# A planned attention-and-MLP kernel: the plan charges VectorE and GpSimd for each other, costs as measured alone, a rank for every unit

## The chip, the cores and the metric

The kernel runs on one core of one Trainium2 chip. The metric is device time in microseconds of one execution; the kernel before was timed three times, with a median of 592.93 us (591.24 to 593.26). The engines are named as the profile names them: PE (TensorE), DVE (VectorE), ACT (ScalarE), POOL (GpSimd), SP (SyncE, which issues the DMAs). PEld is the loading of weights into PE.

## The reference

Attention over 4 batches, 8 heads, 768 positions and 64 channels, with a window of 96 keys and 8 global keys, and then a token-mixing and a channel-mixing MLP.

```python
scores = scale * np.matmul(q, k.transpose(0, 1, 3, 2))
bias = -slopes[:, None, None] * dist[None, :, :]
scores = np.where(keep, scores + bias[None], -1000000000.0)
a = np.exp(scores - np.max(scores, axis=-1, keepdims=True))
a = a / (np.sum(a, axis=-1, keepdims=True) + 1e-09)
x = np.matmul(a, v)            # then heads side by side: (4, 768, 512)
h = np.maximum(xt @ w_tok1, 0.0) @ w_tok2      # xt: x with positions last
u = x + h.transpose(0, 2, 1)
out = u + np.maximum(u @ w_ch1, 0.0) @ w_ch2
```

## The kernel before, in words

All work is cut into units, each for one engine, and a planner writes the order of the units on every engine before the program is built. The program then runs that order: on each engine an instruction follows the one ahead of it in the list (`InOrder`), whatever the others do. The planner (`Plan.record`) goes through time event by event; when an engine is free it gives it, of the units whose predecessors are done and whose buffers and PSUM banks are free, the one with the lowest rank. Each unit carries a cost in microseconds per engine that may do it; where a unit may go to two or three engines, the first that is free takes it. So costs and ranks set two things: the order on each engine, and which engine does a unit that several may do.

The units, with the names of the plan, which the text uses:

- **Attention**, `pair(v)`, v = 0 to 47, 12 for each batch: two heads and 256 positions. `load` (DMA into a ring of four buffers, `e` in the trace), `q` (scaling of the queries), `S` (scores on PE, `sp`), `max` (DVE), `exp` (ACT), `sum` and `inv`, `norm` (POOL, some on DVE), then for v below 20 `T` (transposes on PE, `tp`) and `back` (copy out of PSUM, ACT or DVE), above that `split` (DVE), `turn` (a transposing DMA) and `join`; `V` (values on PE, `op`) and `put` (ACT or DVE). From v = 16 on the load of unit v waits for V of unit v-4, whose buffer it takes.
- **Weights**, `weights(n)`, n = 0 to 29, 64-bit numbers that are turned into a high and a low float: `w` (DMA), `bits` and `down` (ACT), `shift` and `sign` (DVE, rows `t<-w,t`), `high` (ACT), `low` (DVE or POOL, rows `wc<-t,wc`). Only three pieces can be between `bits` and `low` at a time, for they share three buffers (`t`). `w0` to `w5` are for the token MLP, the rest for the channel MLP.
- **Token MLP** of batch b, `tokens(b)`: `N` (transposes, `xtp`), `nh`, `nl`, `J` (`pj`), `jh` (ACT), `jl` (DVE), `U` 0 to 7 (`pu`), `ua` (DVE), `uh` (ACT), `ul` (DVE or POOL). U of batch 0 needs `jl`, and `low3` to `low5`.
- **Channel MLP**, `channel(q)` in chunks of 512 positions with twelve steps each: `F` k (12 matmuls, `hp`), `fh` (ACT, `hh`), `fl` (DVE, `hl`), `g` k in two halves of 6 matmuls (`acc`). This is the dense work, in three matmuls for each product of split floats; the last two chunks are done together in `last()` with fewer products (`P`, `G`, `H`).

Dense work of one batch is laid between the attention units of the next. PSUM has eight banks of 512 floats: `g` holds four, `F` one until `fl` is done, `S`, `T` and `V` two each.

The lines that set the order: the call in `record` that adds a unit's cost (line 212 of the profile's numbering), the `add` calls with their costs in `weights`, `pair`, `tokens` and `channel`, and `rank` with its tables at the end. Before, a rank is a straight line for each kind, as in

```python
    if kind == "pair":
        v = at[0]
        b, i = divmod(v, PER)
        if b == 0:
            return 10.0 * v
        return PAIRS[b - 1][0] + PAIRS[b - 1][1] * i
```

All compute instructions of the trace bear line 235 (`InOrder.__getattr__`), so the rows are told apart by tile names.

Of the kernel before, what the change touches and what calls it, by code (L numbers as in the profile page):

```python
# [22 lines left out]
B, H, S, D = 4, 8, 768, 64  # L23
# [17 lines left out]
FIRST = 3  # L41
PER = H // 2 * NU
# [82 lines left out]
class Plan:  # L125
# [118 lines left out]
class Fast:  # L244
# [68 lines left out]
    def weights(self, n):  # L313
# [5 lines left out]
        add, dve, act = self.plan.add, self.dve, self.act  # L319
# [39 lines left out]
        add(f"w{n}", "sp", 1.85, load, [f"w{n - 1}"] if n else [], rank("load weights", n), ["w", "raw"])  # L359
        add(f"bits{n}", "act", 0.7, bits, [f"w{n}"], r, ["t"])  # L360
        add(f"down{n}", "act", 0.64, down, [f"bits{n}"], r)
        add(f"shift{n}", "dve", 0.73, shift, [f"down{n}"], r)
        add(f"sign{n}", "dve", 0.76, sign, [f"shift{n}"], r, (), ["w", "raw"])
# [38 lines left out]
    def pair(self, v):  # L402
# [130 lines left out]
            if v == FIRST - 1:  # L533
                add("branch", "sp", 0.1, lambda: None, [f"load{v}"], -100)
        if v:
            add(f"q{v}", dict(dve=0.3, act=0.4, pool=0.56) if b == 0 else dict(pool=0.56), 0, lambda e: self.scale(v, e),
                [f"load{v}"], r - PRI['q'])
        wp = ["w"] if wide else ["p", "p"]

# [6 lines left out]
        add(f"sum{v}", *(("pool", 0.37) if FIRST <= v < PER else ("dve", 0.2)), sums, [f"exp{v}0", f"exp{v}1"], r - PRI["sum"])  # L546
        add(f"inv{v}", "dve", 0.16, inverses, [f"sum{v}"], r - PRI["sum"])
        for e in range(2):
            add(f"norm{v}{e}", dict(dve=0.6, pool=1.04) if v < FIRST or PER - 3 <= v < PER else dict(pool=1.4 if b == 1 else 1.04),
                0, lambda en, e=e: norm(e, en), [f"inv{v}"], r - PRI["norm"])  # L550
        if not far:
            add(f"T{v}", "pe", 0.75, transposes, [f"norm{v}0", f"norm{v}1"], r - PRI["T"],
# [4 lines left out]
            late, give = "back", wp + (["w"] if FIRST <= v < PER else [])  # L557
        else:
            for e in range(2):
                add(f"split{v}{e}", "dve", 0.67, lambda e=e: split(e), [f"norm{v}{e}"] + ([f"split{v}0"] if e else []), r - PRI["split"],  # L560
                    [] if e else ["mix", "mix"])
                add(f"turn{v}{e}", "sp", 1.3, lambda e=e: turned(e), [f"split{v}{e}"], -1000)
                add(f"join{v}{e}", dict(act=1.06, dve=0.69), 0, lambda en, e=e: join(e, en), [f"turn{v}{e}"], r - PRI["join"], (), ["p"])
            late, give = "join", ["mix", "mix"]
        add(f"V{v}", "pe", 0.7, values, [f"{late}{v}0", f"{late}{v}1"], r - PRI["V"],
            [("op", v, 0), ("op", v, 1)] + (["w"] if v < H // 2 else ["x"] if b and j == 0 else []), give, "quarters")
        for i in range(2):
            add(f"put{v}{i}", dict(act=0.24, dve=0.25), 0, lambda en, i=i: put(i, en), [f"V{v}"], r - PRI["put"], (), [("op", v, i)])


    def tokens(self, b):
# [83 lines left out]
        for i in range(4 * len(segs)):  # L655
# [10 lines left out]
            add(f"ul{b}{i}", dict(dve=0.12 + w / 900) if b == B - 1 else dict(pool=0.1 + w / 410, dve=0.12 + w / 900), 0, lambda en, i=i: low_u(i, en), [f"uh{b}{i}"],  # L666
                k - PRI['mix'], (), ([] if b == B - 1 else ["x"] if b else ["w"]) if end else [])


    def channel(self, q):  # L670
# [328 lines left out]

def rank(kind, *at):

    if kind == "weights":
        return WEIGHTS[0] + WEIGHTS[1] * at[0] if at[0] < 6 else WEIGHTS[2] + WEIGHTS[3] * at[0]
    if kind == "load weights":
        n = at[0]
        return LOADS[0] + LOADS[1] * n if n < 8 else LOADS[2] + LOADS[3] * n
    if kind == "load":
        return 2.5 * at[0]  # L1010
    if kind == "pair":
        v = at[0]
        b, i = divmod(v, PER)
        if b == 0:
            return 10.0 * v
        return PAIRS[b - 1][0] + PAIRS[b - 1][1] * i
    if kind == "mix":
        b, k = at
        if b == 0:
            return -20.0 + k  # L1020
        return MIXES[b - 1] + 2.5 * k
# [5 lines left out]
LOADS = [10.58, 4.16, 407.44, 1.08]
CHANNEL = [176.2, 6.52]
PAIRS = [(119.72, 6.24), (217.78, 12.78), (353.61, 5.31)]
PRI = {'q': -16.6, 'max': 27.3, 'exp': -7.0, 'sum': 90.7, 'norm': -19.4, 'T': -22.4, 'back': 52.4, 'split': -95.1, 'join': 5.2, 'V': 13.2, 'put': 25.2, 'F': 7.0, 'mix': -9.7, 'hid': 49.7, 'high': 21.0}  # L1030
# [253 lines left out]
```

## Time and profile before

| | before |
|---|---|
| median of 3 runs | 592.93 us |
| the profiled execution | 593.89 us |
| its span, first to last instruction | 592.0 us |
| PE busy | 567.0 us (96%) |
| DVE, ACT, POOL busy | 356.9, 276.2, 234.4 us |
| mean granted TensorE clock | 0.994 |
| moved by DMA | 62.47 MB |

The profile is one execution; the time around its span (593.89 less 592.0) is 1.89 us. A unit's time is found in the trace by its tile name and its place in the order. In a row of the timeline the second number is the time from the start of the first to the end of the last merged instruction; in brackets stands how long the engine had been idle and who released it.

### The profile page before, as it was taken

To read this page: it belongs to the slowest core of one execution; us is meant where nothing else is said; L and a number is where in the kernel's file an instruction comes from. 1 tells how busy PE (TensorE), PEld (TensorE's weight loads), DVE (VectorE), ACT (ScalarE), POOL (GpSimd) and SP (SyncE) were. 2 spreads that over 40 slices of the span, in tenths; PEclk is the share of its full clock that TensorE was granted. 3 is DMA by queue.
4 is the path that set the end of the run, shared out by engine and by line. 5 is a ranking of instruction groups with operands and counts; after the bars stand their busy time and mean duration, and the time that the engine had idled before them with its cause. 6 is when DMAs were issued, how large, how long until landed. Compare 5 with 4: busy or idle time off the path is not lost. (4 is left out here: it accounts for less than half of the span.)

```text
span 592.0 us, 11933 instructions
## 1 busy us (share of the span) xinstructions
PE 567.0 (96%) x4420; PEld 460.4 (78%) x4420; DVE 356.9 (60%) x952; ACT 276.2 (47%) x743; POOL 234.4 (40%) x377
## 2 busy tenths in 40 slices
PE   4989989998999999999999999999999999999995
PEld 2877868777888778788888877787887888888884
DVE  5999998989345664365422487567459755554400
ACT  5999978878433545132322255656244222222000
POOL 3888777656404532060300365344532144410000
PEclk9999999998999999999999999999999999999998
DMA  7990656782301674335420029675100100000201
GB/s 262 372 396 13 224 192 184 260 248 66 92 0 73 115 185 119 45 111 162 69 79 0 1 53 228 158 178 80 29 2 1 71 1 0 1 1 2 77 33 40
DMA packets 62435, 62.47 MB, mean 106 GB/s; under 512 B 46880, under 2 KB 50336, under 8 KB 62368
## 3 DMA queue, kind: packets, MB, share of 16 engines
q1 hardware_dynamic: 62224, 61.62, 36.3%
q8 instruction: 37, 0.61, 0.4%
q14 instruction: 30, 0.25, 0.1%
q10 hardware_dynamic: 144, 0.00, 0.0%
HBM read 44.30 MB, written 6.29 MB: 85 GB/s over the span
## 5 line engine op out<-in xcount | busy, mean ns | idle before, releaser
L235 PE MATMUL acc<-hh,wc 128*128 128x512 f32 x480 | 152.1, 398 | 0.0
L235 PE MATMUL hp<-uh,wc 128*128 128x512 f32 x432 | 144.8, 394 | 0.0
L235 PEld LDWEIGHTS acc<-hh,wc 128*128 128x128 f32 x480 | 88.2, 189 | 21.2 <-issue 2.8
L235 PEld LDWEIGHTS hp<-uh,wc 128*128 128x128 f32 x432 | 81.1, 188 | 18.4 <-ACT x L235 0.6
L235 PE MATMUL acc<-hl,wc 128*128 128x512 f32 x240 | 94.3, 393 | 0.2 <-DVE hl L235 0.2
L235 POOL TENSOR_SCALAR p<-p,st 128x192 f32<-128x192 f32 (+1 forms) x132 | 73.5, 572 | 38.9 <-DVE st L235 19.4
L235 PE MATMUL hp<-ul,wc 128*128 128x512 f32 x216 | 84.3, 390 | 0.0
L235 DVE COPY r<-p 128x768 uint16<-128x768 uint16 x84 | 56.3, 676 | 44.9 <-DMA p<-r 23.0
L235 ACT ACTIVATE hh<-hp 128x512 fp32r<-128x512 f32 x54 | 32.1, 594 | 83.8 <-PE hp L235 82.0
L235 DVE SCALAR_TENSOR_TENSOR hl<-hp,hh 128x512 fp32r<-128x512 f32 x54 | 36.9, 683 | 52.2 <-ACT hh L235 52.0
L235 POOL TENSOR_SCALAR e<-e,sc 128x256 f32<-128x256 f32 x37 | 21.4, 580 | 104.4 <-DMA e<-pk 95.9
L235 ACT ACTIVATE p<-p,st 128x192 f32<-128x192 f32 (+1 forms) x132 | 57.4, 439 | 11.1 <-DVE st L235 11.1
L235 PEld LDWEIGHTS acc<-hl,wc 128*128 128x128 f32 x240 | 45.2, 188 | 10.5 <-DVE hl L235 0.9
L235 DVE SCALAR_TENSOR_TENSOR t<-w,t 128x512 int32<-128x512 int32 x60 | 50.9, 857 | 2.6 <-POOL wc L235 1.3
L235 ACT COPY r<-p 128x768 uint16<-128x768 uint16 x28 | 29.8, 1066 | 37.2 <-DMA p<-r 31.9
L235 PEld LDWEIGHTS hp<-ul,wc 128*128 128x128 f32 x216 | 40.6, 188 | 7.9
L235 PE MATMUL sp<-e 64*64 64x192 f32 (+1 forms) x624 | 33.9, 337 | 12.4 <-ACT e L235 6.1
L235 DVE CUSTOM_DVE_ANT_0 p<-sp,bias 128x192 f32<-128x192 f32 (+1 forms) x132 | 37.3, 342 | 5.3 <-PE sp L235 5.0
L235 PEld LDWEIGHTS sp<-e 64*64 64x64 f32 x624 | 22.6, 141 | 18.8 <-ACT e L235 6.7
L235 PE MATMUL acc<-hid,wc 128*128 128x512 f32 x144 | 33.0, 389 | 0.0
L235 POOL TENSOR_TENSOR o<-uh,ul 128x512 f32<-128x512 f32 x16 | 22.6, 1429 | 25.3 <-DMA out<-o 17.1
L235 POOL TENSOR_TENSOR ul<-x,uh 128x512 fp32r<-128x512 f32 (+1 forms) x14 | 16.2, 1165 | 40.1 <-ACT uh L235 37.5
(145 smaller groups left out, 977.6 us busy)
## 6 DMA issues: line engine op xcount, KB each, us to landing
e<-pk SPq DMA_DIRECT2D x24, 592.0 KB, 4.3
w<-wc SPq DMA_DIRECT2D x24, 512.0 KB, 5.7
e<-pk SPq DMA_DIRECT2D x14, 560.0 KB, 5.0
unit<-pk SPq DMA_DIRECT2D x9, 384.0 KB, 6.2
w<-w SPq DMA_DIRECT2D x6, 512.0 KB, 7.0
out<-o SPq DMA_DIRECT2D x12, 256.0 KB, 2.1
keys<-pk SPq DMA_DIRECT2D x8, 208.0 KB, 5.7
out<-o SPq DMA_DIRECT2D x8, 128.0 KB, 1.8
```

The source lines that it names most:

```text
L235: ins = getattr(self.engine, name)(*args, **kw)
```

## The change

Four things in the planner, and none in what the units do. (1) A unit that starts on DVE while POOL runs one, or the other way round, is charged an extra time (`extra`), if both are in a list of units that share a way to SBUF. (2) The costs of some forty units are replaced: DVE `shift` 0.73 to 0.71, `sign` 0.76 to 0.71, `split` 0.67 to 0.58, POOL `low` 1.45 to 1.33, `norm` 1.04 or 1.4 to 0.88 or 0.98, `base` 1.42 to 1.32, and so on. (3) `rank` takes a number for each unit from a table instead of a straight line, and `TURN`, the weight of a change between the two forms of matmul, goes from 241.81 to 265.19. (4) The priorities of the kinds (`PRI`, `PRI2`) have other values.

```diff
+                more = 0.0
+                side = dict(dve="pool", pool="dve").get(e)
+                if side in running and running[side]["end"] > now:
+                    more = extra(n, e, running[side]["name"], running[side]["end"] - now)
+                running[e] = w
-                end = free[e] = now + w["costs"][e] + best[2]
+                end = free[e] = now + w["costs"][e] + best[2] + more
...
+SHARED = dict(dve=("shift", "sign", "low", "split", "join", "norm", "ul", "base", "td", "tl", "sa", "sb", "sl", "q"),
+              pool=("low", "ul", "base", "sa", "sb", "sl"))
...
+def extra(name, engine, other, left):
+    piece = dict(sa=0.7, sb=0.4) if engine == "pool" else dict(sa=1.4, sb=0.8)
+    left %= piece.get(other[:2], 9.0)
+    if engine == "dve":
+        if not shares(name, "dve"):
+            return 0.0
+        if shares(other, "pool"):
+            return max(0.0, left - 0.1)
+        return 0.15 if name.startswith(("split", "join")) else 0.03
+    if not shares(other, "dve"):
+        return 0.0
+    return min(left, 0.4) if shares(name, "pool") else left
...
-        add(f"low{n}", dict(dve=0.75, pool=1.45), 0, low, [f"high{n}"], r - PRI['high'], (), ["t"])
+        add(f"low{n}", dict(dve=0.71, pool=1.33), 0, low, [f"high{n}"], r - PRI['high'], (), ["t"])
...
-TURN = 241.81
+TURN = 265.19
...
-    if kind == "channel":
-        return CHANNEL[0] + CHANNEL[1] * at[0]
+    return dict(weights=WEIGHTS, loads=LOADS, pair=PAIRS, channel=CHANNEL)[kind][at[0]]
...
-WEIGHTS = [82.59, 11.43, 0.91, 26.98]
+WEIGHTS = [187.43, 202.43, 155.63, 205.62, 247.69, 179.55, 274.1, 257.46, 280.31, 318.63, 390.03, 363.83, 449.84,
...
```

What this does to the order of instructions shows at three places. The names: `e_58` to `e_61` are the four buffers of the attention ring, `p` and `pp` softmax tiles, `t_...` and `w_...` weight pieces under way, `wc` finished weights, `x` the attention's output.

PE from the last U of batch 0 (`pu`) to the first F (`hp`), before:

```order
L235 MATMUL pu<-w2h,pl 128x256
L235 MATMUL op<-p,e_61 64x128 x6
L235 MATMUL op<-p,e_61 64x64 x6
L235 MATMUL sp<-e_59 64x192 x8
L235 MATMUL sp<-e_60 64x192 x8
L235 MATMUL tp<-ident,p 128x128 x6
L235 MATMUL hp<-uh,wc 128x512
```

and in the change, to the units behind that F:

```order
L268 MATMUL hp<-uh,wc 128x512
L268 MATMUL tp<-ident,p 128x128 x6
L268 MATMUL op<-pp,e_60 64x128 x6
L268 MATMUL op<-pp,e_60 64x64 x6
L268 MATMUL op<-p,e_61 64x128 x6
L268 MATMUL op<-p,e_61 64x64 x6
L268 MATMUL sp<-e_59 64x192 x8
```

V14, V15 (`op` from `e_60` and `e_61`), S17 and T16 have moved behind F0, and S18 (`sp` from `e_60`) further still, behind g1.

POOL from the token MLP's `ul` to the scaling of v = 18 and 19 (`e_60`, `e_61`), before:

```order
L235 TENSOR_SCALAR p<-p,st 128x3x64 x4
L235 TENSOR_SCALAR e_60<-e_60,sc 128x256
L235 TENSOR_TENSOR ul<-x,uh 128x512 x2
L235 TENSOR_TENSOR ul<-x,uh 128x256
L235 TENSOR_TENSOR wc<-t_1389,wc 128x512
L235 TENSOR_SCALAR p<-p,st 128x3x64 x8
L235 TENSOR_SCALAR e_61<-e_61,sc 128x256
```

and in the change:

```order
L268 TENSOR_TENSOR ul<-x,uh 128x256
L268 TENSOR_TENSOR wc<-t_1395,wc 128x512
L268 TENSOR_TENSOR wc<-t_1426,wc 128x512
L268 TENSOR_SCALAR e_60<-e_60,sc 128x256
L268 TENSOR_SCALAR e_61<-e_61,sc 128x256
L268 TENSOR_SCALAR p<-p,st 128x3x64 x4
```

Before, q19 (`e_61`) stands behind the eight `norm` instructions of v = 17 and 18; now q18 and q19 stand together ahead of the `norm` of v = 17.

ACT ahead of fh of step 7 (`hh`), before:

```order
L235 CAST wc<-t_2147 128x512
L235 ACTIVATE w_2137<-w_2137 128x512
L235 CAST wc<-t_2186 128x512
L235 ACTIVATE t_2235<-w_2145 128x512
L235 ACTIVATE hh<-hp 128x512
```

and in the change:

```order
L268 ACTIVATE t_2144<-w_1973 128x512
L268 COPY r<-p 128x2x384
L268 CAST wc<-t_2004 128x512
L268 ACTIVATE w_1973<-w_1973 128x512
L268 ACTIVATE hh<-hp 128x512
```

Before, a `bits` (`t_...`), which must find one of the three buffers free, stands right ahead of `hh`; now three instructions that take no buffer lie between them.

## Rows read from the trace of the kernel before

**Rows 1.** The page: span, and busy us, share and instructions of each engine.
```profile
span 592.0 us, 11933 instructions
PE 567.0 (96%) x4420; PEld 460.4 (78%) x4420; DVE 356.9 (60%) x952; ACT 276.2 (47%) x743; POOL 234.4 (40%) x377
```

**Rows 2.** Windows by stage: busy us and (xcount) of PE, PEld, DVE, ACT, POOL; clock, DMA.
```profile
0.00:20.00 20.00, 11.43 (x130) 8.12 (x134) 12.17 (x71) 12.97 (x49) 9.34 (x43) 1.00 0.86 299
20.00:60.00 40.00, 36.69 (x649) 30.53 (x642) 38.67 (x156) 37.88 (x133) 35.19 (x75) 1.00 0.65 241
60.00:140.00 80.00, 75.54 (x675) 60.24 (x675) 73.36 (x168) 66.74 (x163) 51.87 (x56) 0.98 0.62 208
140.00:340.00 200.00, 200.00 (x1470) 164.39 (x1469) 95.45 (x264) 73.73 (x192) 59.95 (x95) 1.00 0.33 81
340.00:420.00 80.00, 78.47 (x732) 60.45 (x730) 53.66 (x178) 43.51 (x137) 40.10 (x73) 1.00 0.62 134
420.00:460.00 40.00, 39.77 (x226) 33.42 (x226) 27.47 (x41) 16.66 (x34) 14.92 (x15) 1.00 0.00 1
460.00:585.00 125.00, 125.00 (x552) 103.21 (x551) 55.40 (x80) 24.72 (x40) 23.04 (x23) 1.00 0.07 24
585.00:592.00 7.00, 0.14 (x1) 0.00 (x0) 0.76 (x2) 0.00 (x0) 0.00 (x0) 0.74 0.14 44
```

**Rows 3.** PE's timeline around S19, and POOL's ahead of it.
```profile
88.84 1.53 PE L235 MATMUL sp<-e 64*64 64x192 f32 x32 [1.28 <-POOL e L235]
...
81.51 6.35 POOL L235 TENSOR_SCALAR p<-p,st 128x192 f32<-128x192 f32 x8 [4.10 <-ACT p L235]
```

**Rows 4.** Timeline of 128 to 140: ACT, DVE and PE around step 7.
```profile
132.41 0.69 ACT L235 ACTIVATE t<-w 128x512 int32<-128x512 uint8 x1 [0.52 <-POOL wc L235]
132.99 0.58 ACT L235 ACTIVATE hh<-hp 128x512 fp32r<-128x512 f32 x1
...
134.05 0.68 DVE L235 SCALAR_TENSOR_TENSOR hl<-hp,hh 128x512 fp32r<-128x512 f32 x1
...
134.78 1.55 PE L235 MATMUL sp<-e 64*64 64x192 f32 x14 [2.10 <-DVE hl L235]
```

**Rows 5.** Windows of 2 us behind that stall, columns as in rows 2.
```profile
134.00:136.00 2.00, 1.22 (x14) 0.78 (x14) 1.97 (x4) 1.93 (x4) 1.14 (x1) 0.60 0.08 31
136.00:138.00 2.00, 2.00 (x10) 1.41 (x6) 2.00 (x8) 1.02 (x4) 0.72 (x2) 0.55 0.00 0
```

**Rows 6.** Groups by shape, DVE and ACT: busy us, mean ns of one.
```profile
L235 DVE COPY pp<-tp 128x384 f32<-128x384 f32 x18 | 9.4, 544 | 0.0
L235 DVE COPY x<-op 128x128 f32<-128x128 f32 x43 | 11.2, 281 | 16.2 <-PE op L235 16.2
...
L235 ACT CAST wc<-t 128x512 fp32r<-128x512 f32 x24 | 14.9, 620 | 5.2 <-DVE t L235 4.9
```

**Rows 7.** Timelines of POOL and DVE, one beside the other.
```profile
72.31 3.68 POOL L235 TENSOR_TENSOR ul<-x,uh 128x512 fp32r<-128x512 f32 x3
76.13 1.28 POOL L235 TENSOR_TENSOR wc<-t,wc 128x512 fp32r<-128x512 f32 x1
...
73.73 1.67 DVE L235 SCALAR_TENSOR_TENSOR t<-w,t 128x512 int32<-128x512 int32 x1
75.32 2.37 DVE L235 TENSOR_TENSOR ul<-x,uh 128x256 fp32r<-128x256 f32 x2
...
84.33 2.04 DVE L235 SCALAR_TENSOR_TENSOR t<-w,t 128x512 int32<-128x512 int32 x3
```

**Rows 8.** The attention ring's loads of 60 to 100: landing time, and one issue.
```profile
DMA to landing us min/median/max: 3.4/4.3/5.1
...
75.00 6.38 SPq L235 DMA_DIRECT2D e<-pk  x2
```

**Rows 9.** The chain that ended last: start us, us, what; a V and an F.
```profile
384.29 0.83 PE op L235 x32
...
386.70 2.72 PE hp L235 x12
```

More of the change, by code (lines that the diff above doesn't have):

```diff
@@ L155, in record @@
         free = {e: self.busy.get(e, 0.0) for e in self.LATENCY}
+        running = {}
         ready = {e: [] for e in free}
@@ L224, in record, with shares @@
                 w["run"]()
+SHARED = dict(dve=("shift", "sign", "low", "split", "join", "norm", "ul", "base", "td", "tl", "sa", "sb", "sl", "q"),
+              pool=("low", "ul", "base", "sa", "sb", "sl"))
+def shares(name, engine):
+    kind = name.rstrip("0123456789_")
+    if engine == "dve":
+        return kind in SHARED["dve"] or name[:4] in ("fl12", "fl21", "fl22")
+    return kind in SHARED["pool"]
+def extra(name, engine, other, left):
+    piece = dict(sa=0.7, sb=0.4) if engine == "pool" else dict(sa=1.4, sb=0.8)
+    left %= piece.get(other[:2], 9.0)
+    if engine == "dve":
+        if not shares(name, "dve"):
[6 more added lines that the diff above has]
+    return min(left, 0.4) if shares(name, "pool") else left
 class InOrder:
@@ L358, in weights @@
         r = rank("weights", n)
-        add(f"w{n}", "sp", 1.85, load, [f"w{n - 1}"] if n else [], rank("load weights", n), ["w", "raw"])
+        add(f"w{n}", "sp", 1.85, load, [f"w{n - 1}"] if n else [], rank("loads", n), ["w", "raw"])
         add(f"bits{n}", "act", 0.7, bits, [f"w{n}"], r, ["t"])
         add(f"down{n}", "act", 0.64, down, [f"bits{n}"], r)
-        add(f"shift{n}", "dve", 0.73, shift, [f"down{n}"], r)
-        add(f"sign{n}", "dve", 0.76, sign, [f"shift{n}"], r, (), ["w", "raw"])
+        add(f"shift{n}", "dve", 0.71, shift, [f"down{n}"], r)
+        add(f"sign{n}", "dve", 0.71, sign, [f"shift{n}"], r, (), ["w", "raw"])
         add(f"high{n}", "act", 0.55, high, [f"sign{n}"], r - PRI['high'], ["w"] if n >= 6 else [])
-        add(f"low{n}", dict(dve=0.75, pool=1.45), 0, low, [f"high{n}"], r - PRI['high'], (), ["t"])
+        add(f"low{n}", dict(dve=0.71, pool=1.33), 0, low, [f"high{n}"], r - PRI['high'], (), ["t"])
     def load(self, v):
@@ L535, in pair @@
         if v:
-            add(f"q{v}", dict(dve=0.3, act=0.4, pool=0.56) if b == 0 else dict(pool=0.56), 0, lambda e: self.scale(v, e),
+            add(f"q{v}", dict(dve=0.33, act=0.45, pool=0.51) if b == 0 else dict(pool=0.51), 0, lambda e: self.scale(v, e),
                 [f"load{v}"], r - PRI['q'])
@@ L548, in pair @@
         for e in range(2):
-            add(f"norm{v}{e}", dict(dve=0.6, pool=1.04) if v < FIRST or PER - 3 <= v < PER else dict(pool=1.4 if b == 1 else 1.04),
+            add(f"norm{v}{e}", dict(dve=0.56, pool=0.88 if j else 0.98) if v < FIRST or PER - 3 <= v < PER else dict(pool=0.88 if j else 0.98),
                 0, lambda en, e=e: norm(e, en), [f"inv{v}"], r - PRI["norm"])
@@ L559, in pair @@
             for e in range(2):
-                add(f"split{v}{e}", "dve", 0.67, lambda e=e: split(e), [f"norm{v}{e}"] + ([f"split{v}0"] if e else []), r - PRI["split"],
+                add(f"split{v}{e}", "dve", 0.58, lambda e=e: split(e), [f"norm{v}{e}"] + ([f"split{v}0"] if e else []), r - PRI["split"],
                     [] if e else ["mix", "mix"])
                 add(f"turn{v}{e}", "sp", 1.3, lambda e=e: turned(e), [f"split{v}{e}"], -1000)
-                add(f"join{v}{e}", dict(act=1.06, dve=0.69), 0, lambda en, e=e: join(e, en), [f"turn{v}{e}"], r - PRI["join"], (), ["p"])
+                add(f"join{v}{e}", dict(act=1.02, dve=0.64), 0, lambda en, e=e: join(e, en), [f"turn{v}{e}"], r - PRI["join"], (), ["p"])
             late, give = "join", ["mix", "mix"]
@@ L567, in pair @@
         for i in range(2):
-            add(f"put{v}{i}", dict(act=0.24, dve=0.25), 0, lambda en, i=i: put(i, en), [f"V{v}"], r - PRI["put"], (), [("op", v, i)])
+            add(f"put{v}{i}", dict(act=0.24, dve=0.28), 0, lambda en, i=i: put(i, en), [f"V{v}"], r - PRI["put"], (), [("op", v, i)])
     def tokens(self, b):
@@ L1002, in rank @@
 def rank(kind, *at):
[L1004 to L1008, printed above, removed]
     if kind == "load":
         return 2.5 * at[0]
[L1011 to L1016, printed above, removed]
@@ L1017, in rank @@
-    if kind == "mix":
[L1018 to L1021, printed above, removed]
-    if kind == "channel":
-        return CHANNEL[0] + CHANNEL[1] * at[0]
-WEIGHTS = [82.59, 11.43, 0.91, 26.98]
[L1027 to L1030, printed above, removed]
@@ L1031 @@
-PRI2 = {'early': 159.0, 'quad': 34.3, 'mixed': 108.7, 'second': -69.0, 'step': -14.4, 'tail': -66.4}
-MIXES = [154.62, 92.38, 36.73]
+    if kind == "mix":
+        return MIXES[at[0]][at[1]]
+    return dict(weights=WEIGHTS, loads=LOADS, pair=PAIRS, channel=CHANNEL)[kind][at[0]]
+WEIGHTS = [187.43, 202.43, 155.63, 205.62, 247.69, 179.55, 274.1, 257.46, 280.31, 318.63, 390.03, 363.83, 449.84,
+    445.14, 566.63, 619.17, 632.75, 732.88, 771.19, 718.2, 778.68, 897.77, 721.26, 928.92, 936.19, 1046.95, 1023.45,
+    1052.01, 1272.87, 1233.9]
@@ new lines @@
+LOADS = [10.75, 13.69, 17.75, -36.63, 26.33, -23.75, 175.28, 342.66, 246.0, 9.66, -129.27, -40.8, -72.02, 319.45,
+    231.54, 358.73, 360.25, 207.17, 135.45, 75.85, 123.24, 231.7, 11.13, 135.28, 30.29, 77.81, 4.77, -133.29, -15.95,
+    97.32]
+CHANNEL = [211.28, 216.11, 170.58, 180.73, 232.04, 249.28, 266.07, 264.82, 336.71, 299.75, 264.34, 325.31, 327.89,
[3 rows of a table added]
+PAIRS = [80.09, 53.65, -8.56, 5.75, -24.94, 105.58, 44.93, 73.16, 116.75, 140.02, 133.92, 104.06, 79.74, 90.14,
+    108.45, 127.73, 180.89, 166.41, 179.23, 184.63, 221.95, 204.85, 239.0, 223.66, 286.47, 296.95, 360.35, 351.35,
+    396.57, 392.72, 465.65, 416.51, 444.91, 464.49, 566.07, 495.83, 150.35, -31.61, -51.4, 104.04, -161.68, -141.97,
+    -225.81, -69.02, -115.17, -286.86, 2.71, -3.9]
@@ L1035, in fast @@
+PRI = {'q': -190.81, 'max': 31.44, 'exp': -35.66, 'sum': 198.81, 'norm': -105.05, 'T': 29.7, 'back': 77.81,
+    'split': 42.61, 'join': 119.23, 'V': -16.0, 'put': 88.55, 'F': 17.92, 'mix': 41.47, 'hid': 58.93, 'high': 98.87}
+PRI2 = {'early': 219.13, 'quad': -13.17, 'mixed': -188.2, 'second': 194.01, 'step': 295.68, 'tail': -258.52}
+MIXES = [[65.77, 85.4, -42.46, 43.21, -101.22, -6.98, 8.16, -18.51, 61.62, 8.86, 19.41, -19.45, 16.47, 29.51],
[4 rows of a table added]
 @with_exitstack
```

4 lines of the change are left out of this document (2 added, 2 removed), and 7 rows, old and new, of tables (CHANNEL, MIXES).

## The prediction

> **What bounds the kernel now.** First the busy times: PE works 567.0 of 592.0 us, and no other engine more than 60% [rows 1]. So no change of order can give more than PE's 25.0 us of idleness, and the question is where these lie. The windows by stage tell it, 20.00 or 80.00 being the length and the next number PE's busy time [rows 2]. In 0 to 20 PE is idle for 8.57 us, most of it before the first loads are in; in 20 to 60 for 3.31, in 60 to 140 for 4.46, in 140 to 340 not at all, in 340 to 420 for 1.53, in 420 to 460 for 0.23, in 460 to 585 not at all, and behind 585, where the last sums are stored, for 6.86. The reader is to see that the same rows name the partner: in 20 to 60 DVE is busy for 38.67 of 40 us and ACT for 37.88, in 60 to 140 DVE for 73.36 of 80; behind 140 both have room. PE waits where DVE and ACT are full, and the clock falls there too (0.98 in 60 to 140).
>
> Two single waits make up most of 60 to 140. S19 waits 1.28 us for POOL, which has just run eight norm instructions in 6.35 us with the scaling of v = 19 behind them [rows 3]. And a score unit (S22 or S23) waits 2.10 us for `hl`, that is for the bank of F7: `hl` (134.05) follows `hh` on ACT (132.99), `hh` stood behind a `bits` that waited 0.52 us for a buffer which POOL's `low` gives back, although F7 was long done [rows 4]. Behind that stall the granted clock is 0.60 for two microseconds and 0.55 for the next two, about the lower of the two levels, 1.2 of 2.4 GHz, and PE is at half speed [rows 5].
>
> **The change part by part.** What each unit computes is untouched, and PE's matmuls are the same in number and kind. The sum is made against the profiled execution, 593.89 us, which is 0.96 above the median of 592.93.
>
> *Start and tail: nothing.* PE's order is the same up to T3, and the last stores come behind the last matmul as before. The 8.57 and the 6.86 stay; their cover is that nothing else is left to run there.
>
> *S19: minus 1.3.* POOL now scales v = 18 and 19 ahead of the norm of v = 17, and S19 stands behind g3 on PE. The 1.28 has no cause any more. What is late next is the norm of v = 17, for which see below.
>
> *The stall at step 7: minus 3.5.* Ahead of `hh` there are now three instructions that take no buffer, and PE has V21 besides both halves of g6 between F7 and the scores. So the 2.10 goes. With it goes the low clock: 2.00 us at 0.55 lose 0.90, and 1.22 busy us at 0.60 lose 0.49, together 1.4 [rows 5]. The bounds are 0 (a `bits` still stands four places ahead, and may still wait for POOL) and 3.5; I take all, since the row shows only 0.52 of ACT waiting to start it [rows 4].
>
> *The small waits of 20 to 140: minus 2.1.* The idle 3.31 and 4.46, less 1.28 and 2.10, leave 4.4 us of short waits of T, V and S. In DVE's order 119 units stood up to the second `jl` of batch 0, now 110. Much of that is only put off (shift, sign, max). What leaves DVE: six `back` against two, four times 0.544, or 2.2; one `low` fewer, taken as long as the `hl` of the same size, 0.68; what comes are three `put` more, 0.8 [rows 4, 6]. Net 2.1. As DVE is full, that much of PE's waiting can go. Against it, ACT gets the four `back` and is as full. The bounds are 0 and 4.4; 2.1 lies in the middle.
>
> *340 to 460: minus 0.9.* The scores of the last batch now start one to two dense steps sooner, right behind U27, so that the same chain of softmax, transposing DMA and values has more F and g beside it. Of the idle 1.8 I take half; bounds 0 and 1.8 [rows 2].
>
> *New waits: plus 1.9.* U00 stood behind `jl`; now `high4` follows `jh` on ACT (0.62) and POOL's `low4` (1.28) follows that, 1.9 in place of some 0.7 for `jl` [rows 4, 6, 7]. PE has four units between J05 and U00, as before, so between 0 and 1.2 shows: 0.6. And some wait of the size of S19's will be new in an order in which nearly every unit has another neighbour: 1.3; the bounds are 0 and, as in rows 4 and 5, 3.5.
>
> *F0 sooner: nothing by itself.* It comes ahead of V14, V15, S17, S18 and T16; they are done later, and PE's sum is the same. It gives cover, counted above.
>
> Sum: 1.3 + 3.5 + 2.1 + 0.9 = 7.8 less, 1.9 more, net 5.9. That is 588.0 by the profiled execution and **587.0** by the median.
>
> **The new charge itself.** The trace bears it out in kind. Beside POOL's two-input `ul` (72.31 to 75.99) a DVE shift-or-sign took 1.67 us and two small `ul` 2.37; beside norms, with one input, three of the same DVE instructions took 2.04, or 0.68 each [rows 3, 7]. So DVE loses about a microsecond beside the former and nothing beside the latter, as the plan now says.
>
> The Trainium skill, page "SBUF — State Buffer", section "Who interferes with whom", says that a DVE instruction with two SBUF inputs contends with any GpSimd instruction that reads SBUF, and that whichever comes first holds the pair for its whole length while the other stops. The norms read SBUF and are not in the plan's list for POOL, so by that rule the plan leaves out waits; the 2.04 us speak against the rule for them, and the measurement decides. By the rule the sum would be the fourth rival's, by the row it is the one above.
>
> **The rivals.**
>
> *First, slower: POOL in front of the ring.* load18 and load19 need the buffers of V14 and V15, which now come behind F0, and on POOL q18 and q19 stand ahead of the norm of v = 17; if a load is late, that norm waits too, and T17, and all of PE behind it. From V15 to T17 PE has S17, V16, F1, three halves of g, F2: 2 x 0.83 + 2 x 2.72 + 3 x 1.36 = 11.2 us (a half of g has half of F's matmuls) [rows 9]. The load takes 4.3, at most 5.1, and six POOL instructions at up to 0.79 another 4.8, so 9.1 to 9.9 [rows 3, 8]. For it: a ring load sat in SP's queue for most of 6.38 us [rows 8]. Against it: 1.3 us of slack at the worst landing. It decides from a landing 6.4 us behind V15. If it comes at T17, and again at the next two units whose buffers come late, each costs what rows 4 and 5 show, 3.5: 10.5 more, against 7.8 less and the 0.6 of U00, so 3.3 more: 596.2 by the median. Chance 0.19.
>
> *Second, no change: waits move.* In 20 to 60 DVE, ACT and POOL are busy for 38.67, 37.88 and 35.19 of 40 us [rows 2]. If PE's waits are their sum of work, a better order only moves them. Then 592.9, give or take 1.8. Against it: behind 60 POOL has a third of its time free, and the stall at step 7 was a matter of order. Chance 0.15.
>
> *Third, faster: all waits go.* The plan now knows the durations and the waits between DVE and POOL; if its order holds, 3.31 + 4.46 + 1.53 + 0.23 = 9.5 of idleness and 1.4 of clock go, 10.9: 582.0. Against it: every unit's start must hold to some tenths of a microsecond. Chance 0.16.
>
> *Fourth, the plan charges too little.* Were DVE held up beside norms as beside `ul`, by half a norm or 0.4, and a third of the 60 shift and sign lay beside one, 8 us of DVE time would be missing from the plan, where DVE is busy for 73.36 of 80 us [rows 2, 3]. The second and third gain, 5.6, would be gone: 592.6, no change. That the charge does not do what it says is this case too. The 2.04 us speak against it [rows 7]. Chance 0.04.
>
> **How the numbers follow.** The forecast has 0.46, with a range of its own of 583 to 590.5 (the small waits at 4.4 and no new wait; or the stall still there). About 0.3%, 1.8 us, is what a measurement of this kernel can tell from no change. Faster by more: forecast 0.45, third 0.16, second 0.02, fourth 0.01, together 0.64. Within: 0.01 + 0.11 + 0.03 = 0.15. Slower: first 0.19, second 0.02, together 0.21. The range reaches from just below the third rival to just above the first, 581.5 to 597.
>
> **What would show it.** Right: PE's idle time in 20 to 140 near 4 us instead of 7.8; no score unit that waits for `hl` over 1 us; a granted clock of 1.00 throughout; dense work at 100% from 140 on; DVE's `t<-w,t` below its present mean. Wrong: T17 or another T waiting for POOL's `p` with POOL waiting for the ring's DMA; a new dip of the clock; or PE idle as before, at other units.

## The result and the profile after

The changed kernel takes **585.78 us** (median of 7 runs, 585.31 to 586.83), the kernel before 591.56 beside it (7 runs, 589.18 to 593.98): a ratio of 0.9901, 95% interval 0.9877 to 0.9925. So it is faster by 5.8 us of the medians. The forecast was 587.0, 5.9 under the median known then. The profiled execution took 586.52 us with a span of 584.6; that of before 593.89 and 592.0. The spans differ by 7.4.

The page of the changed kernel, busy times, which answer to [rows 1]:

```profile
PE 562.3 (96%) x4420; PEld 457.9 (78%) x4420; DVE 350.5 (60%) x948; ACT 277.1 (47%) x746; POOL 239.5 (41%) x378
```

PE's idle time is 584.6 less 562.3, or 22.3, against 25.0; its busy time is 4.7 shorter with the same 4420 matmuls. The windows by stage, columns as in [rows 2] (length, busy us and count of PE, PEld, DVE, ACT, POOL, clock, DMA):

```profile
0.00:20.00 20.00, 11.86 (x178) 8.58 (x180) 13.36 (x77) 13.70 (x52) 10.64 (x47) 1.00 0.84 303
20.00:60.00 40.00, 37.52 (x624) 30.25 (x624) 37.31 (x146) 39.10 (x129) 34.44 (x69) 1.00 0.69 259
60.00:140.00 80.00, 78.85 (x688) 64.71 (x687) 72.85 (x176) 68.58 (x174) 58.93 (x69) 1.00 0.65 206
140.00:340.00 200.00, 199.35 (x1489) 163.44 (x1488) 101.01 (x292) 78.83 (x219) 68.51 (x115) 1.00 0.33 81
340.00:420.00 80.00, 76.64 (x745) 59.81 (x744) 45.70 (x141) 38.99 (x111) 35.05 (x53) 1.00 0.53 125
420.00:460.00 40.00, 40.00 (x189) 33.61 (x188) 30.15 (x46) 13.85 (x29) 9.77 (x7) 1.00 0.07 25
460.00:577.00 117.00, 117.00 (x518) 96.89 (x517) 49.37 (x71) 24.02 (x39) 22.19 (x23) 1.00 0.05 17
577.00:585.00 8.00, 1.12 (x5) 0.58 (x4) 0.76 (x2) 0.00 (x0) 0.00 (x0) 0.75 0.13 40
```

Between 20 and 140 PE is idle for 2.48 and 1.15, together 3.63, where it was 7.77; the clock is 1.00 there. In 340 to 420 it went the other way, from 1.53 to 3.36, and in 140 to 340 there is 0.65 of idleness where there was none.

The same is seen from places where the same work lies behind PE in both orders. The first transposes of the second batch's token MLP (N10), before and after:

```profile
155.54 1.69 PE L235 MATMUL xtp<-ident,x 128*128 128x128 f32 x14
```

```profile
147.13 1.91 PE L268 MATMUL xtp<-ident,x 128*128 128x128 f32 x16
```

PE is 8.4 us ahead at N10 and 7.4 at the end. So **all of the gain lies ahead of 150 us, and about 1 us of it is given back behind**. Both kernels have run the same 1568 matmuls up to there; PE was busy with them for 139.20 us before and 135.36 after. So of the 8.4 us 4.6 were idle time and 3.8 came out of PE's busy time.

What is left of waiting between 20 and 140, PE's groups by line with the idle time before them and who ended it:

```profile
L268 PE MATMUL sp<-e 64*64 64x192 f32 (+1 forms) x192 | 10.3, 324 | 0.0
L268 PE MATMUL tp<-ident,pp 128*128 128x128 f32 x72 | 10.2, 279 | 0.7 <-POOL pp L268 0.7
L268 PE MATMUL op<-pp,unit 64*64 64x128 f32 (+1 forms) x280 | 8.7, 248 | 1.4 <-DVE pp L268 0.7 <-issue 0.5 <-ACT pp L268 0.2
...
L268 PE MATMUL tp<-ident,p 128*128 128x128 f32 x30 | 4.3, 274 | 0.2 <-POOL p L268 0.2
L268 PE MATMUL op<-r,e 64*64 64x128 f32 (+1 forms) x64 | 2.2, 250 | 0.9 <-ACT r L268 0.9
```

No score unit of the ring (`sp<-e`) waits at all, neither for `hl` nor for a scaling on POOL. Of the T units one waits 0.67 us at 22.23 (`tp<-ident,pp`), and one 0.22 at 87.14 (`tp<-ident,p`). The two single waits of [rows 3, 4] are gone, and the longest that is left in these 120 us is 0.93, of V21 for its join (`op<-r,e`).

The new waits lie in the last batch's attention. PE's timeline there:

```profile
365.14 0.99 PE L268 MATMUL op<-r,e 64*64 64x128 f32 x30 [0.71 <-DVE st L268]
367.26 0.98 PE L268 MATMUL sp<-e 64*64 64x192 f32 x16 [1.13 <-DVE st L268]
...
398.24 0.90 PE L268 MATMUL op<-r,e 64*64 64x128 f32 x32 [1.03 <-DVE st L268]
```

and the chain of waits that leads to the first of these (start us, us, what):

```profile
351.50 5.25 DMA out<-o
...
356.89 0.15 POOL o L268
...
358.13 2.20 POOL p L268 x4
...
361.22 2.75 DMA p<-r
...
364.04 0.27 ACT r L268
```

V42 at 365.14 needs the join on ACT, which begins at 364.04 and took 1.05; the join needs a transposing DMA of 2.75; that needs a split that needs four norms on POOL; and the norms stand on POOL behind an output sum (`o`) that was held for the store of an earlier one (POOL was idle for 7.45 us before it). One late buffer of the output thus goes through POOL's order into the attention. S40 at 367.26 starts when its scaling on POOL ends (366.73 and 0.48, after 5.20 of waiting for the ring's load); the row names DVE's `st`, which ended at the same time, so which of the two held it longer can't be told. The third row, V45 at 398.24, was not followed back.

### The profile page after: what moved, and what is told of

Its sections match the earlier page's. It is cut to its first block, busy times and chain, and to the rows that moved or that the text cites. A ratio compares the mean times of both kernels' runs of the same rounds, so it can differ in the third digit from the quotient of the medians.

```text
span 584.6 us, 11977 instructions
## 1 busy us (share of the span) xinstructions
PE 562.3 (96%) x4420; PEld 457.9 (78%) x4420; DVE 350.5 (60%) x948; ACT 277.1 (47%) x746; POOL 239.5 (41%) x378
## 4 chain that ended last, share of the span: by engine, by line
PE 71%; DMA 11%; POOL 8%; DVE 3%; issue 3%; ACT 2%; SPq 2%; POOLq 0%; DVEq 0%; ACTq 0%
PE acc L268 28%; PE hp L268 26%; PE pj L268 5%; PE pu L268 4%; DMA e<-pk 4%; DMA p<-r 4%; POOL p L268 4%; PE op L268 3%; PE sp L268 3%; DMA w<-w 2%; POOL pp L268 2%; PE xtp L268 1%; ACT pp L268 1%; DMA out<-o 1%; DVE p L268 1%
## 5 line engine op out<-in xcount | busy, mean ns | idle before, releaser
L268 PE MATMUL hp<-uh,wc 128*128 128x512 f32 x432 | 142.5, 393 | 0.2 <-PE sp L268 0.2
L268 POOL TENSOR_SCALAR p<-p,st 128x192 f32<-128x192 f32 (+1 forms) x132 | 77.8, 607 | 30.4 <-DVE st L268 15.6
L268 DVE SCALAR_TENSOR_TENSOR t<-w,t 128x512 int32<-128x512 int32 x60 | 47.6, 806 | 1.6 <-issue 1.3
L268 ACT COPY r<-p 128x768 uint16<-128x768 uint16 x27 | 28.5, 1067 | 36.4 <-DMA p<-r 24.0
L268 POOL TENSOR_TENSOR wc<-t,wc 128x512 fp32r<-128x512 f32 x19 | 26.6, 1402 | 14.8 <-ACT wc L268 14.6
## 6 DMA issues: line engine op xcount, KB each, us to landing
e<-pk SPq DMA_DIRECT2D x24, 592.0 KB, 4.3
```

The lines of the kernel that those rows point to most:

```text
L268: ins = getattr(self.engine, name)(*args, **kw)
```

## The experiments

The theories for the first four: **A**, ranks, costs and charge make this order only together, and each part alone gives another order with other waits; **B**, the charge alone brings the gain; **C**, the ranks alone do. For the others: **D**, a wait that is taken from PE is gone; **E**, it comes back at another place; **F** and **G** are told where they are expected. A ratio is to the kernel before, run beside it.

### The parts alone

*The charge alone*, the kernel before with `running` and `extra`, old costs and ranks:

```diff
...
-                end = free[e] = now + w["costs"][e] + best[2]
...
+                end = free[e] = now + w["costs"][e] + best[2] + more
...
```

> Before, with the charge for DVE and POOL alone; costs and ranks as before. Theory A (an order is good where ranks, costs and charge were found together; any of them alone gives another order with other waits): 590 to 596, PE idle in 20 to 140 us still 6 to 9 us. Theory B (knowing the waits at SBUF is what helps, whatever the ranks): 587 to 589, PE idle in 20 to 140 near 5 us, the mean of DVE's t<-w,t below 0.82 us.

Measured: 596.45 us, ratio 1.0068 (1.0047 to 1.0089).

*Charge and costs*, the old ranks:

```diff
+                end = free[e] = now + w["costs"][e] + best[2] + more
...
+        add(f"low{n}", dict(dve=0.71, pool=1.33), 0, low, [f"high{n}"], r - PRI['high'], (), ["t"])
```

> Before, with the charge and the new costs, and the old straight-line ranks. Theory A: 589 to 596, no better than before beyond 0.5%. Theory B: 586 to 588, nearly all of the gain. If the ranks alone carry the gain (theory C): 591 to 593.

Measured: 601.88 us, ratio 1.0162 (1.0108 to 1.0215).

*The ranks alone*, with `PRI`, `PRI2` and `TURN`, old costs and no charge:

```diff
-TURN = 241.81
+TURN = 265.19
...
+WEIGHTS = [187.43, 202.43, 155.63, 205.62, 247.69, 179.55, 274.1, 257.46, 280.31, 318.63, 390.03, 363.83, 449.84,
```

> The changed kernel's ranks and priorities with the old costs and no charge. Theory C (the ranks alone carry it): 585 to 587. Theory A: 588 to 594, a part of the gain or none, with waits of 1 us or more at places where the changed kernel has none. Theory B: 591 to 594.

Measured: 600.68 us, ratio 1.0160 (1.0123 to 1.0197).

*The changed kernel without the charge*:

```diff
-                    more = extra(n, e, running[side]["name"], running[side]["end"] - now)
+                    more = 0.0
```

> The changed kernel without the charge; new costs and ranks stay. Theory A: 587 to 592, worse than the changed kernel by 2 us or more, since the ranks were found with the charge. Theory B: 589 to 592. Theory C: 585 to 587, no difference.

Measured: 613.14 us, ratio 1.0359 (1.0323 to 1.0395). Windows of 20 to 140 for the four in the order above, for the first two also of 140 to 460:

```profile
20.00:140.00 120.00, 115.42 (x1363) 92.78 (x1362) 106.22 (x319) 108.93 (x310) 82.72 (x132) 1.00 0.66 223
140.00:460.00 320.00, 317.25 (x2394) 256.33 (x2386) 181.81 (x475) 132.64 (x359) 104.62 (x169) 1.00 0.34 82
```

```profile
20.00:140.00 120.00, 115.34 (x1297) 92.58 (x1294) 103.17 (x312) 106.83 (x302) 86.78 (x133) 1.00 0.67 220
140.00:460.00 320.00, 315.00 (x2403) 255.99 (x2402) 180.37 (x481) 123.92 (x344) 109.72 (x171) 0.99 0.34 83
```

```profile
20.00:140.00 120.00, 111.64 (x1268) 90.40 (x1264) 114.32 (x333) 107.39 (x300) 81.60 (x124) 0.99 0.59 210
```

```profile
20.00:140.00 120.00, 111.49 (x1271) 89.49 (x1268) 112.67 (x315) 105.26 (x291) 85.23 (x126) 0.97 0.62 217
```

The reader is to see the second number. With the charge and the old ranks PE is idle for 4.6 us in 20 to 140, where the whole change has 3.63, and yet the program is slower, since more is lost behind. In 140 to 460, where the kernel before had 1.76 us of idleness, these two have 2.75 and 5.00; in 460 to 577 PE is busy for 113.5 and 112.1 us of 117, with a clock of 0.97 and 0.96. Each of the four is slower than the kernel before, by 4 to 21 us, so theories B and C fall by the time. Two signs of B did come in the first run: idle time near 5 us and a mean of `t<-w,t` below 0.82 us (0.811, table below); they did not bring the time. A's word that each part alone gives another order with other waits holds, but its numbers do not: all four times lie above every range that was set down, the last by 21 us, and in the first run A had 6 to 9 us of idle time.

### Single waits, taken out of the kernel before

Here the finished order is edited: a unit is taken out of the list and put in ahead of another.

```diff
             assert not left, left
+        for n, ahead in [('fh_7', 'bits26')]:
+            self.order.remove(n)
+            self.order.insert(self.order.index(ahead), n)
```

> Before, with its order unchanged but for one unit on ACT: fh of step 7 moved ahead of the bits of weight piece 26. Theory D (the single waits are worth what the prediction's sum put on them): the wait of a score unit for hl and the low clock behind it go, 3.5 us less, ratio 0.994. Rival E (the waits of 20 to 140 us come from full engines and only move): the same time within 1 us, with another wait of 1 to 2 us between 130 and 140 us, the weight piece being late instead.

Measured: 591.53 us, ratio 0.9996 (0.9982 to 1.0011). The stall did not go:

```profile
132.13 0.62 ACT L238 CAST wc<-t 128x512 fp32r<-128x512 f32 x1 [1.40 <-DVE t L238]
132.66 0.59 ACT L238 ACTIVATE hh<-hp 128x512 fp32r<-128x512 f32 x1
```

```profile
127.53 5.17 DVE L238 SCALAR_TENSOR_TENSOR t<-w,t 128x512 int32<-128x512 int32 x5 [0.51 <-issue]
132.79 0.69 DVE L238 TENSOR_TENSOR wc<-t,wc 128x512 fp32r<-128x512 f32 x1
133.40 0.68 DVE L238 SCALAR_TENSOR_TENSOR t<-w,t 128x512 int32<-128x512 int32 x1
134.00 0.68 DVE L238 SCALAR_TENSOR_TENSOR hl<-hp,hh 128x512 fp32r<-128x512 f32 x1
```

```profile
134.74 0.94 PE L238 MATMUL sp<-e 64*64 64x192 f32 x14 [2.20 <-DVE hl L238]
```

In the kernel before the same stretch of DVE began so:

```profile
127.75 5.17 DVE L235 SCALAR_TENSOR_TENSOR t<-w,t 128x512 int32<-128x512 int32 x5 [0.51 <-issue]
```

The first two rows are ACT's, then DVE's and PE's. `hh` is now right behind a `high` that waited 1.40 for DVE, and `hl` stands behind a `low` and a `sign`. It begins at 134.00, in the kernel before at 134.05 [rows 4]. So the `bits` and its buffer, which the prediction named, were not the cause. DVE was: five shift-or-sign instructions took 5.17 us in both kernels, 1.03 each, with two of POOL's `low` beside them, where three took 2.04 beside norms [rows 7], and `hl` comes two places behind them. At the pace of those three, five would take 3.4, so some 1.8 us, nearly the whole stall, is by this estimate the wait between DVE and POOL that the new charge is about.

The scaling of v = 19 ahead of the norms of v = 17, so that S19 no longer waits:

```diff
+        for n, ahead in [('q19', 'norm170')]:
```

> Before, with one unit moved on POOL: the scaling of v = 19 ahead of the norm of v = 17. Theory D: S19 no longer waits, 1.3 us less, ratio 0.998. Rival E: no change, T17 or V17 waits instead, since the scaling waits for its load and holds up the norm.

Measured: 591.36 us, ratio 0.9985 (0.9970 to 1.0001). POOL's rows and PE's:

```profile
80.03 6.35 POOL L238 TENSOR_SCALAR p<-p,st 128x192 f32<-128x192 f32 x8 [0.81 <-ACT p L238]
86.36 0.99 POOL L238 TENSOR_SCALAR e<-e,sc 128x256 f32<-128x256 f32 x1
```

```profile
87.41 0.88 PE L238 MATMUL sp<-e 64*64 64x192 f32 x16 [0.68 <-POOL e L238]
```

The same eight norms in 6.35 us stand now ahead of the scaling of v = 20, and S20 waits: half of the wait has moved on by one unit. The interval holds D's 0.998 and E's 1, so the time does not decide between them.

Both moves together:

```diff
+        for n, ahead in [('fh_7', 'bits26'), ('q19', 'norm170')]:
```

> Before, with both units moved. Theory D: 4.8 us less, ratio 0.992, which would be most of the changed kernel's gain. Rival E: within 1 us of before.

Measured: 591.84 us, ratio 1.0008 (0.9991 to 1.0025). The stall is there (2.06), but behind it the clock did not fall. Windows of 2 us, as in [rows 5]:

```profile
134.00:136.00 2.00, 1.60 (x17) 1.17 (x18) 1.97 (x3) 1.66 (x3) 1.52 (x1) 1.00 0.00 0
136.00:138.00 2.00, 1.53 (x7) 0.98 (x6) 2.00 (x12) 1.32 (x4) 0.72 (x2) 1.00 0.00 0
```

At last the stall with its real cause, on both engines: `fh_7` and `fl_7` ahead of the weight that stands in their way.

```diff
+        for n, ahead in [('fh_7', 'high24'), ('fl_7', 'low24')]:
```

> The kernel before with two units moved in the finished order: ScalarE's fh_7 in front of high24 and VectorE's fl_7 in front of low24, so that nothing of a weight's preparation stands between U70 and the scores that wait for hl of step 7. The run with fh_7 moved alone left the stall of 2.1 us at 134.8, because hl on VectorE stood behind low24 and sign25. Theory D (the stall is a matter of the two orders at that place and is worth what it shows): PE's wait for hl falls from 2.1 to under 0.5, the time by 1.6 to 3.5 (2.1 and up to 1.4 of clock): 588.4 to 590.3 beside a before of 591.9, ratio 0.994 to 0.997. Theory E (a wait that is taken from PE comes back at the next group that is short of something, here weights 24 and 25 that come later): PE's idle time between 20 and 140 and behind it keeps its sum, ratio 0.999 to 1.001.

Measured: 589.92 us, ratio 0.9981 (0.9965 to 0.9997), or 1.1 us faster (0.2 to 2.1); by the medians, with 591.88 beside it, 2.0. PE's rows:

```profile
132.58 0.87 PE L238 MATMUL sp<-e 64*64 64x192 f32 x14 [0.90 <-DVE hl L238]
...
135.76 0.47 PE L238 MATMUL hp<-uh,wc 128*128 128x512 f32 x1 [0.71 <-DVE st L238]
```

and the window of 20 to 140:

```profile
20.00:140.00 120.00, 111.90 (x1271) 89.97 (x1270) 109.79 (x314) 104.40 (x296) 85.45 (x128) 1.00 0.62 219
```

The wait for `hl` falls from 2.10 to 0.90, and 3 us later PE waits 0.71 for DVE, which has its shift and sign still to do. So 0.5 of the 2.1 is gone from these rows. By the ratio the time gains 1.1 where D had 1.6 to 3.5 and E at most 0.6; by the medians it lies in D's range. But E's sign came too: PE is idle in 20 to 140 for 8.10 us, before for 7.77, V21 alone waiting 0.96 for 0.45. So the run stands between the two, and where its time was won its profiled execution does not show.

### Single waits, taken out of the changed kernel

```diff
+        for n, ahead in [('g7_0', 'V21'), ('load40', 'turn420'), ('max440', 'join451'), ('max441', 'join451'), ('F42', 'V45')]:
```

> The changed kernel with five units moved by hand, where its trace shows PE waiting: g7's first half ahead of V21, load40 ahead of turn420, max of v = 44 ahead of the second join of v = 45, F42 ahead of V45. Theory D: PE's waits of 0.93 (V21), 1.13 (S40) and 1.03 us (V45) go, 2 to 3 us less than the changed kernel, 583 to 584 where before is 592. Rival E: as the changed kernel, within 1 us.

Measured: 588.85 us, ratio 0.9948 (0.9928 to 0.9969), so slower than the changed kernel. Then the first of these moves alone:

```diff
+        for n, ahead in [('g7_0', 'V21')]:
```

> The changed kernel with one unit moved in the finished order: g7_0 in front of V21, as in the run of the changed kernel with four moves, which had 0.8 us less idle time between 60 and 140 and 3.1 more between 340 and 420. Theory D (each wait is worth what it shows): the wait of V21 at 125.1 (0.93 for the join) goes, 340 to 420 stays at 3.4 idle: 585.0, ratio 0.988 to 0.989 to before. Theory E (the waits move): 585.4 to 586.5, ratio 0.9895 to 0.991, with as much idle time in other places.

Measured: **584.62 us**, ratio 0.9886 (0.9861 to 0.9911). The windows of 60 to 140 and 340 to 420, first with all moves, then with the one:

```profile
60.00:140.00 80.00, 79.67 (x686) 65.36 (x681) 73.08 (x175) 68.48 (x175) 58.73 (x69) 1.00 0.65 206
...
340.00:420.00 80.00, 73.51 (x719) 56.77 (x718) 45.02 (x139) 36.92 (x107) 31.72 (x51) 0.98 0.52 124
```

```profile
60.00:140.00 80.00, 79.81 (x706) 65.40 (x706) 73.02 (x181) 68.74 (x176) 60.22 (x73) 1.00 0.66 210
...
340.00:420.00 80.00, 76.37 (x737) 59.14 (x736) 44.80 (x141) 38.25 (x109) 33.13 (x52) 0.98 0.52 125
```

The move ahead of V21 takes 1.0 us of idleness out of 60 to 140 and gives 0.3 back later, as D has it. The moves that were meant to free V42, S40 and V45 brought 3 us of new waits in their place, as E has it. With the one move the kernel is faster than before, and by the medians the fastest of all; its interval and that of the changed kernel (0.9877 to 0.9925) overlap, so that it beats that one too is not shown.

### The same planner with a hundredth of a microsecond

One cost of the changed kernel, `high` on ACT, from 0.55 to 0.56, which tells the plan nothing about the chip, but changes PE's order from near its start on:

```diff
-        add(f"high{n}", "act", 0.55, high, [f"sign{n}"], r - PRI['high'], ["w"] if n >= 6 else [])
+        add(f"high{n}", "act", 0.56, high, [f"sign{n}"], r - PRI['high'], ["w"] if n >= 6 else [])
```

> The changed kernel with one cost changed by 0.01 us, high from 0.55 to 0.56, which is less than the spread of that instruction in the trace and says nothing new of the chip, but gives another order from the first tenth of the program on. Theory A, in its sharper form F (what the change gains belongs to this one order, which was picked among many, and the charge and the ranks have no worth of their own): 588 to 602, ratio 0.994 to 1.017, PE's idle time between 20 and 140 over 5 and new waits behind 340. Theory G (the charge and the costs make the planner's forecast right, so any order that it makes with them is as good): 584.5 to 587.5, ratio 0.988 to 0.992.

Measured: 595.96 us, ratio 1.0071 (1.0047 to 1.0094). And `put` on DVE:

```diff
-            add(f"put{v}{i}", dict(act=0.24, dve=0.28), 0, lambda en, i=i: put(i, en), [f"V{v}"], r - PRI["put"], (), [("op", v, i)])
+            add(f"put{v}{i}", dict(act=0.24, dve=0.29), 0, lambda en, i=i: put(i, en), [f"V{v}"], r - PRI["put"], (), [("op", v, i)])
```

> A second sample of the same: the changed kernel with put on VectorE at 0.29 for 0.28. Theory F: 588 to 602, ratio 0.994 to 1.017, other waits than with high at 0.56. Theory G: 584.5 to 587.5, ratio 0.988 to 0.992.

Measured: 598.51 us, ratio 1.0118 (1.0090 to 1.0146). Windows, first of `high`, then of `put`:

```profile
20.00:140.00 120.00, 113.49 (x1314) 90.89 (x1309) 104.59 (x308) 106.46 (x303) 89.87 (x138) 0.99 0.68 227
140.00:460.00 320.00, 315.43 (x2370) 252.90 (x2369) 177.60 (x477) 131.13 (x357) 106.15 (x170) 0.99 0.32 81
```

```profile
20.00:140.00 120.00, 112.62 (x1251) 91.52 (x1248) 103.52 (x304) 104.55 (x297) 80.21 (x124) 0.97 0.59 211
140.00:460.00 320.00, 313.47 (x2426) 253.71 (x2425) 180.75 (x488) 133.54 (x360) 112.69 (x180) 0.99 0.36 87
```

With the full charge, the new costs and all the new ranks, a hundredth more in one cost takes 10 to 13 us away: PE is idle in 20 to 140 for 6.5 and 7.4 us and not for 3.63, and the clock falls again. G falls, and F's forecast came in both: what the change gains belongs to this one order. That the order was picked among many, as F also says, no run shows. Nor does any show whether ranks that are searched for anew with the charge would beat ranks searched for without it; both the kernel before and the changed one may be the best of such a search, and then any step away from either loses.

Does the charge do anything, then? The mean of DVE's 60 shift-or-sign instructions (`t<-w,t`), of which a part waits for POOL, tells it:

| kernel | charge | mean, ns | time, us |
|---|---|---|---|
| before | no | 857 | 591.56 |
| ranks alone | no | 833 | 600.68 |
| changed, no charge | no | 870 | 613.14 |
| charge alone | yes | 811 | 596.45 |
| charge and costs | yes | 830 | 601.88 |
| high 0.56 | yes | 810 | 595.96 |
| put 0.29 | yes | 836 | 598.51 |
| changed | yes | 806 | 585.78 |

With it the mean is 819 over the five kernels, without 853 over the three: 35 ns less, or 2 us of DVE time over 60. Each is one execution, and the two sets touch (836 and 833); but in the two pairs that differ by the charge alone it falls by 46 and 64 ns. So the charge seems to lower the waiting that it describes, by a little, and the time does not follow it.

## Why the prediction was right, and where not

**The sum was right: 5.9 less forecast, 5.8 less by the medians.** Its terms were right in part, and that they add up is in part luck. The profiled executions, 7.4 apart, give for each term:

| term | forecast, us | between the two profiles |
|---|---|---|
| S19 | -1.3 | -1.3 |
| stall at step 7, wait | -2.1 | -2.1 |
| stall at step 7, clock | -1.4 | -1.4 |
| small waits of 20 to 140 | -2.1 | -0.8 |
| 340 to 460 | -0.9 | +1.6 |
| new waits (measured: 140 to 340) | +1.9 | +0.65 |
| start and tail | 0 | -0.8 |
| the rest of PE's busy time | 0 | -3.3 |
| sum | -5.9 | -7.4 |

*What bounds the kernel.* The place was right: the gain came in 20 to 140, with 3.63 us of idleness left where about 4 were foretold, a clock of 1.00, and no time won behind 140, where PE was full. The limit was not: PE's idle time was said to be all that an order can give, and 4.7 of the 7.4 us came out of its busy time.

*S19 and the stall at step 7.* Both waits are gone, as foretold, but their prices as single waits are not borne out. Taken out of the kernel before, the first gave 0.9, for S20 then waits; between 1.8 gained and 0.1 lost, this can be told neither from 1.3 nor from nothing. For the second, 1.2 of the 2.1 us was taken away and gave 1.1 (0.2 to 2.1) where 3.5 was reckoned for all of it. The step that failed is the reading of one row [rows 4]: that ACT had waited 0.52 us for a buffer was taken for the cause of `hl` being late. The engine that was behind was DVE, and its own rows of the 7 us ahead, 1.03 us for each shift and sign, would have told it. The 1.4 of clock belonged to the profiled execution; a stall as long was without it in another.

*The small waits.* They were 4.4 beside the two large ones and are 3.6, new ones included. The room on DVE came nearly as reckoned: its work in 20 to 140 fell from 112.0 us to 110.2, 1.9 less for 2.1. That PE's waits would fall by as much did not come out.

*340 to 460: wrong in sign.* The idle time is 3.36 against 1.53 and 0.23. The step said that scores that start sooner have more dense work beside them. It left out that the norms of that stage stand in POOL's order behind output sums, and that V42 hangs on store, norm, split, transposing DMA and join in a row.

*New waits.* 0.65 in 140 to 340; the waits of 340 to 420 are new too, but stand already in the term above. U00, for which 0.6 was set down, does not wait: no `pu` is among the groups that wait.

*Start and tail.* The difference is no more than one program shows: over the kernel before and the four edits of its order, which leave the start as it is, PE's idle time in the first 20 us was 7.4 to 8.6 (here 8.6 and 8.1), and behind the last matmul 6.4 to 7.3 (here 6.9 and 6.5).

*Busy PE.* Foretold were 1.4 us less, from the clock; the page shows 4.7. The number of matmuls and of changes between their two forms (91) is the same in both traces. Taken from one matmul's start to the next, idle time left out, score units took 2.2 us less, value units 1.6, F and g 1.75, the rest 0.9 more (the clock's 1.4 is among these), and 3.9 of the 4.7 lie between 20 and 140. A matmul's record reaches past the start of the next (0.39 us where starts are 0.23 apart, in `pj` behind 150 us), so a short wait between two does not show as idle. That the order took away such short waits too would fit; what held these matmuls no row names, and it stays open.

*The rivals.* The first, POOL in front of the ring's loads, did not come: the T unit at 87.14 waits for 0.2 us. The second, waits that move, did not come for the change as a whole, but it is what three of the six runs that edit the finished order show (the scaling, the stall on both engines, the five moves together). The third, that all waits go, did not come: 7.6 us of idleness are left between 20 and 460. The fourth, norms that hold DVE, did not come either, but the prediction gave a wrong reason for it. DVE beside norms in the changed kernel:

```profile
131.63 1.28 DVE L268 SCALAR_TENSOR_TENSOR t<-w,t 128x512 int32<-128x512 int32 x2
```

POOL's four norms of that time, and four later with no shift or sign beside them:

```profile
131.73 2.90 POOL L268 TENSOR_SCALAR p<-p,st 128x192 f32<-128x192 f32 x4 [1.14 <-DVE x L268]
...
367.60 1.64 POOL L268 TENSOR_SCALAR p<-p,st 128x192 f32<-128x192 f32 x4 [0.39 <-ACT p L268]
```

DVE's two took 1.28, 0.64 each, not held at all. The first of the four norms, which began 0.10 us behind them, took 1.40 of the 2.90, where the four at 367.60 took 0.41 each: it ended 0.22 behind DVE's two. So POOL pays here. The eight norms of [rows 3] took 0.79 each, so they paid too, and the prediction read in its 2.04 us only DVE's half. The Trainium skill, page "SBUF — State Buffer", section "Who interferes with whom", says that a DVE instruction with two SBUF inputs contends with a GpSimd instruction that reads SBUF, and that issue order decides who blocks. With DVE first, the trace agrees; the 2.04 us do not speak against the rule, as the prediction has it. With a norm first, DVE lost little: a shift or sign that began at 119.51, while a norm ran, took 0.83 for 0.68. The planner has this too. `extra` does not ask, as the words on the change have it, that both units be listed: a POOL unit outside POOL's list is charged all that is left of a listed DVE unit (`else left`), and a listed DVE unit beside a POOL unit outside the list 0.15 or 0.03. So the plan does not leave these waits out, as the prediction says it would.

The same section says that copies in a two-port mode contend too. Whether this kernel's copies run in that mode no row shows, but a DVE copy (`r<-p`, 128x768) took 1.64 us beside POOL's `low` of 1.29, and 0.61 at 124.78, where POOL was idle:

```profile
120.67 1.64 DVE L268 COPY r<-p 128x768 uint16<-128x768 uint16 x1 [0.33 <-POOL p L268]
...
124.78 0.61 DVE L268 COPY r<-p 128x768 uint16<-128x768 uint16 x1 [1.87 <-DMA p<-r]
```

```profile
120.60 1.29 POOL L268 TENSOR_TENSOR wc<-t,wc 128x512 fp32r<-128x512 f32 x1
```

**What was not asked before predicting** is how much two orders of one planner differ by nothing. The six made here from parts of the change, or from the change with a hundredth added, lie between 595.96 and 613.14; the kernel before and the changed one are both below all six. Against such a spread an argument from the charge's truth carries little. The forecast went by the rows of this very order, and came out as far as these go and with the luck told above.

## What to carry to other kernels

Where a planner writes the order, judge the order it gives and not its rules: with the old ranks the charge made the kernel 4 us slower, and 10 with the measured costs beside it; a cost changed by 0.01 us made the changed kernel 10 to 13 us slower. Time such a change beside perturbations of itself before its gain is put down to its idea. And price a wait on a full engine by a run that removes it, since its row shows where work was missing, and not what comes back when it is moved.

## What the runs showed of the hardware

The clock does not always fall behind the same stall. Behind 2.10 us of waiting it was 0.60 and 0.55 in the next two windows of 2 us [rows 5], which is half speed, 1.2 of 2.4 GHz, for most of that time; with the scaling moved and a stall of 2.15 it was 0.56 and 0.59; with `fh_7` moved and 2.20 it was 0.86 and 0.50; with both moves and 2.06 it stayed at 1.00. The kernel before spread over 4.8 us in its seven runs and the changed kernel, which has no stall of that kind, over 1.5; but with one unit of it moved the spread was 3.5 and with five 5.9. Over the 64 runs of the kernel before that stood beside the experiments, the mean granted clock hardly goes with the time (correlation -0.04, -0.13 and -0.25 in the three sets). So that the clock makes the spread is not shown.

DVE and POOL held each other up here in either order: behind POOL's `ul` a shift or sign took 1.67 us for 0.68 [rows 7], and behind two of DVE's a norm of POOL took 1.40 for 0.41.
